# Seven raw weight buffers and eleven split ones, splits at most six steps ahead, load buffers at multiples of 256 bytes

## The chip, the cores and the metric

The kernel runs on one core of a Trainium2 chip. Its time is that of one execution in device microseconds; several executions are timed and the median is given. Below, PE is TensorE, DVE is VectorE, ACT is ScalarE, POOL is GpSimd and SP is the engine whose queue issues most DMA transfers.

## The reference

Linear attention over 8 batches and 8 heads (576 tokens, 64 values a head, 128 features), whose 4,608 rows of 512 values then go through a mixture of experts (MoE): a skip gate, the best of 8 experts for each row that passes it, and two matrix products with a ReLU between them.

```python
def phi(x):
    proj = np.einsum('bhsd,df->bhsf', x, w_phi)
    proj = proj - np.max(np.abs(proj), axis=-1, keepdims=True)
    return np.concatenate([np.exp(proj), np.exp(-proj)], axis=-1)
q_p, k_p = (phi(q), phi(k))
kv = np.einsum('bhsf,bhsd->bhfd', k_p, v)
z = np.sum(k_p, axis=2)
num = np.einsum('bhsf,bhfd->bhsd', q_p, kv)
den = np.einsum('bhsf,bhf->bhs', q_p, z)[..., None] + 1e-06
attn = num / den
...
do_compute = x @ w_skip > 0
xc = x[do_compute]
e_idx = np.argmax(xc @ w_gate, axis=1)
h = np.maximum(xc[mask] @ w1[e], 0.0)          # for each expert e, mask = its rows
y[mask] = gate_w[mask, None] * (h @ w2[e])
out[do_compute] = xc + y
```

Everything is fp32. A product of two fp32 matrices is made on PE of three products: each operand is split into a high part (`hi`, a copy rounded to PE's fp32r type) and the low rest (`lo` = value − `hi`), and hi·hi, hi·lo and lo·hi are summed.

## The kernel before

**Attention** takes the first 404 us or so. For each batch and pair of heads, q, k and v come in by SP's DMAs (`raw`, `v` and `vt`), DVE transposes part of the input (`xTt`, L301), PE makes the features, and the finished rows leave from `xm` (or `xt`) to the DRAM array `xrows` and to the output. A program's SBUF is handed out pool by pool in the order in which the pools are opened; attention's pools are closed before the MoE's open, so that the MoE's buffers lie over attention's.

**The MoE** works through ten slots, in the order E, E, E, C, C, S beside C, C, D beside S, C, D. E and D hold 256 rows, C 192, S 128. For each slot eight chunks of 512 KB of weights go past: four of w1, with which the slot's hidden values are made, and four of w2, with which its outputs are. One slot with one chunk is a *step*, 96 in all, numbered in PE's order. What happens to chunk k:

- **Load.** `fetch` (L181) issues one DMA on SP's queue (L188 for w1, L191 for w2) into one of four raw buffers, number k mod 4. So load k waits until the split of chunk k−4 has read its buffer.
- **Split.** `split` (L194) takes one of twelve pairs, number k mod 12: ACT copies the chunk to the high half (L199), and then DVE in one instruction, or POOL in four, subtracts to make the low half (L204). It waits until PE has finished step k−12.
- **Use.** `mm1` (L903, L916, L917, L919: w1) or `mm2` (L922 on, L930: w2), for S slots `half1` and `half2` (L855).

Around a step lies other work. `gather_rows` (L217) fetches a slot's rows from `xrows` by a POOL transfer; `rows` turns them on PE (L790) and ACT and DVE make their high and low halves (L793, L794). Hidden values are split by ACT (L808, L818) and DVE (L809, L820); for C slots ACT and DVE first empty the PSUM bank into `hsum` (L908, L909); for S slots ACT makes `hr` (L838) and PE turns it (L844). At a slot's end DVE makes the output rows `o` (L877, L888, L889) and their indices `si` (L862), and POOL scatters them (L863). Hidden values have three PSUM banks (`ps_P`) and one more (`ps_K`), transposes two (`ps_U`), outputs two (`ps_O`).

Each engine works through its queue in order. The order is written out by hand, in the loop over steps: at step k the loop first emits the splits that are due, each with the load of the chunk four further, and then step k's products. How far ahead splits go is set by a small planner (`T`, `ready`, `parted`), which estimates when a step starts and when a chunk has been loaded and split:

```python
while nxt < len(steps) and nxt <= k + 8 and (nxt <= k + 1 or parted[nxt] <= T[k] + 1.0):
```

So a split stands at most eight steps ahead of its use. Which engine subtracts is fixed: DVE, except for chunks 1 and 3 of w1 of a C slot, chunks 1 and 3 of an S slot, and a list for the E slots, which are POOL's.

Of the kernel before, what the change touches and what calls it, by code (L numbers as in the profile page):

```python
# [8 lines left out]
F32 = mybir.dt.float32  # L9
F32R = mybir.dt.float32r  # L10
BF16 = mybir.dt.bfloat16
I32 = mybir.dt.int32
# [5 lines left out]

P = 128
SLOT = 256  # L20
CFG = {'late': 1, 'gp': (0, 1, 2, 4, 6, 8, 9, 11, 12, 14, 17, 19, 21), 'rows': 9.0, 'tab': (2, 4, 5, 6, 6, 7, 8, 9, 10, 11, 12, 13, 16, 20, 32), 'ql': -2, 'q1': 0, 'vtl': 3, 'at': 6, 'cp': 0, 'ini': 'vvpvppvvpvp', 'inz': '', 'seq': ('E', 'E', 'E', 'C', 'C', 'SC', 'C', 'DS', 'C', 'D'), 'lag': (1, 3, 4, 5, 6), 'post': (4, 5, 7), 'man': (8, 79), 'dnow': 0, 'off': 6, 'order': 'EPAZUT', 'direct': (), 'nb': {'K': 1, 'P': 3, 'U': 2, 'O': 2}, 'apools': (('ld', 2), ('hl', 5), ('up', 5), ('zp', 2), ('ep', 7), ('kvp', 6), ('ac', 1), ('xp', 2)), 'mpools': (('rawp', 1), ('mx', 2), ('wseta', 1), ('mo', 2), ('wsetb', 1), ('wsetc', 1))}


@with_exitstack
def kernel(
# [13 lines left out]
    B, H, S, D = q.shape  # L39
    NF = w_phi.shape[1]  # L40
    E = w_gate.shape[1]
# [22 lines left out]
    const = ctx.enter_context(tc.tile_pool(name="const", bufs=1))  # L64
# [5 lines left out]
    pools = {}  # L70
    for nm, bufs in CFG["apools"]:
        pools[nm] = actx.enter_context(tc.tile_pool(name=nm, bufs=bufs))
    ac = pools["ac"]
    NB = CFG["nb"]
    DIRECT = CFG["direct"]

# [9 lines left out]
    nc.vector.memset(warm, 0.0)  # L86
    nc.scalar.activation(out=warm, in_=warm, func=AF.Exp)

    wsrc = ac.tile([P, NF], F32, name="wsrc")
    own = ac.tile([P, 2], F32, name="own")  # L90
    nc.vector.memset(own, 0.0)
    for dh in range(2):
        for hd in range(2):
# [17 lines left out]
    ones_f = const.tile([P, 32], F32, name="ones_f")  # L111
    iota_p = const.tile([P, P], F32, name="iota_p")

    vts = [ac.tile([P, 2, 2, D], F32, name="vt%d" % j) for j in range(2)]
    for vt in vts:
        nc.gpsimd.memset(vt, 0.0)
    desc = const.tile([P, E], F32, name="desc")
# [9 lines left out]
    eid0 = const.tile([1, 3], I32, name="eid0")  # L127
    idg0 = const.tile([P, 3, 2], I32, name="idg0")
    pad0 = const.tile([P, 3, 2], I32, name="pad0")
    mark = const.tile([1, 1], I32, name="mark")  # L130

    ft = const.tile([P, NSL, 4], I32, name="ft")

# [42 lines left out]
    wpool = []  # L176
# [2 lines left out]
    NFC = FF // FC  # L179

    def fetch(which, wap, c):  # L181
        rawp = wpool[0]
        i = nchunk[0]
        nchunk[0] += 1
        raw = rawp.tile([P, 1024], F32, tag="wraw%d" % (i % 4), name="wraw_c", bufs=1)
        if which == 1:
            src = wap[:, :, c * FC:(c + 1) * FC].rearrange("o (k p) f -> p (o k) f", p=P)
            nc.sync.dma_start(out=raw.rearrange("p (k f) -> p k f", f=FC), in_=src)  # L188
        else:
            src = wap[:, c * FC:(c + 1) * FC, :].rearrange("o (k p) m -> p (o k) m", p=P)  # L190
            nc.sync.dma_start(out=raw.rearrange("p (k m) -> p k m", m=DM), in_=src)  # L191
        return which, i, raw

    def split(chunk, eng):  # L194
        which, i, raw = chunk
        s = i % 12
        pair = wpool[1 if s < 4 else 2 if s < 9 else 3].tile([P, 2, 1024], F32R, tag="w%d" % s, name="w", bufs=1)
        hi, lo = pair[:, 0], pair[:, 1]
        nc.scalar.activation(out=hi, in_=raw, func=AF.Copy)  # L199

        n = 256 if eng is nc.gpsimd else 1024
        for a in range(0, 1024, n):
            r = slice(a, a + n)
            eng.tensor_tensor(out=lo[:, r], in0=raw[:, r], in1=hi[:, r].bitcast(F32), op=ALU.subtract)  # L204
        w = FC if which == 1 else DM
        return hi.rearrange("p (k f) -> p k f", f=w), lo.rearrange("p (k f) -> p k f", f=w)
# [24 lines left out]
    with actx:  # L231
        ld, hl, zp, up, ep, kvp, xp = (pools[nm] for nm in ("ld", "hl", "zp", "up", "ep", "kvp", "xp"))
# [55 lines left out]
        def st_t(u, i):  # L288
# [13 lines left out]
            else:  # L302
                nc.vector.transpose(out=xT.rearrange("p (g q c) -> p q g c", g=4, q=4), in_=src)
            nc.scalar.activation(out=hi, in_=xT, func=AF.Copy)  # L304
            nlo[0] += 1
            (nc.vector if CFG["ini"][nlo[0] - 1:nlo[0]] == "v" else nc.gpsimd).tensor_tensor(  # L306
                out=lo, in0=xT, in1=hi.bitcast(F32), op=ALU.subtract)
            u.hlp[(i + 1) // 2] = (hi, lo)

        def st_proj(u, i):  # L310
# [14 lines left out]
            if u.kind == "k" and i in DIRECT:  # L325
                nm = small.tile([P, 4], F32, tag="nm", name="nm")
                nc.vector.tensor_scalar(out=nm, in0=m, scalar1=-1.0, scalar2=None, op0=ALU.mult)
                u.u[i] = (pv, m, nm)
                if CFG["dnow"]:
                    st_exp_k(u, i)  # L330
# [9 lines left out]
        def st_exp_k(u, i):  # L340
# [22 lines left out]
            nz[0] += 1  # L363
            zeng = nc.vector if CFG["inz"][nz[0] - 1:nz[0]] == "v" else nc.gpsimd
            zeng.tensor_tensor(out=z, in0=e[:, 0:2, :], in1=e[:, 2:4, :], op=ALU.add)  # L365
# [343 lines left out]
        n = len(streams[0][0])  # L709
# [32 lines left out]
        man = None  # L742
        for t in range(n + OFF + LA):
            if CFG["man"] and t == CFG["man"][0]:
                man = ExitStack()
# [30 lines left out]
    pools = {}  # L776
    for nm, bufs in CFG["mpools"]:
        pools[nm] = ctx.enter_context(tc.tile_pool(name=nm, bufs=bufs, reuse_waits="tile"))
    wpool += [pools[x] for x in ("rawp", "wseta", "wsetb", "wsetc")]
    mxp, mo = pools["mx"], pools["mo"]  # L780

    def split_rows(xg, pad):
# [319 lines left out]
    def weight_regs(e):  # L1102
        r = nc.sync.value_load(e, min_val=0, max_val=E - 1)
        return bass.ds(r, 1)
# [3 lines left out]
    steps = []  # L1108
    cnt = dict(start)
    for grp in CFG["seq"]:  # L1110
# [7 lines left out]
        for which, w, n in how:  # L1118
            for _ in range(n):
                x = slots[which]  # L1120
# [7 lines left out]
    order = sorted(begin, key=begin.get)  # L1128
    raws, wts = {}, {}

    def load(k):
        if k < len(steps):
            w, x, c = steps[k]
            if w == 1 and c == 0:
                kind, i = x
                regs[x] = weight_regs((eid0 if kind == "E" else eid)[0:1, i:i + 1])
            raws[k] = fetch(w, (w1, w2)[w - 1][regs[x]], c)

    def part(k, eng):
        if k < len(steps):  # L1140
            wts[k] = split(raws.pop(k), eng)
# [11 lines left out]
    FIRST = 4  # L1153
    LATE = CFG["late"]
    took = {"E": 2.85, "D": 2.85, "C": 2.4, "S": 1.45}
    T, ready, parted = [], [], []
    for k, (w, x, c) in enumerate(steps):
        arrive = 0.0 if k < FIRST else max(ready[k - 1] + (3.0 if k < 12 else 2.35), parted[k - 4] + 4.0)
        ready.append(arrive)
        parted.append(max(arrive, T[k - 12] + 3.0 if k >= 12 else 0.0, parted[k - 1] + 1.25 if k else 0.0))  # L1160
        T.append(max(T[k - 1] + took[steps[k - 1][1][0]] + (1.0 if w == 1 and c == 0 else 0.0) if k else 2.0,
                     parted[k] + 2.5))

# [6 lines left out]
    def at(k, f):  # L1170
        along.append((k, f))
# [32 lines left out]
    with tc.manual_schedule():  # L1204
        nxt = FIRST
        for k in range(FIRST, FIRST + 4):
            load(k)
        rests[1]()
        for k, (w, x, c) in enumerate(steps):
            kind, i = x  # L1210
            for f in [f for s, f in before if s == k]:
                f()
            tabled[0] = kind != "E"
            todo = [f for s, f in along if s == k]
            while nxt < len(steps) and nxt <= k + 8 and (nxt <= k + 1 or parted[nxt] <= T[k] + 1.0):
                w_, x_, c_ = steps[nxt]
                v = nxt not in CFG["gp"] if x_[0] == "E" else not (
                    (x_[0] == "C" and w_ == 1 or x_[0] == "S") and c_ % 2 == 1)
                part(nxt, nc.vector if v else nc.gpsimd)
                load(nxt + 4)  # L1220
                nxt += 1
            if w == 1:
                if kind == "S":
                    st = hss.setdefault(x, {})
                    half1(wts[k], xss[x], c, st)
                    if c % 2 == 1:
                        st[c // 2] = half1_out(st[c // 2], c // 2)

                        def turn(st=st, g=c // 2):
                            st[g] = half1_turn(st[g])  # L1230
                        at(k + 1, turn)
                else:
                    hss.setdefault(x, []).append(mm1(wts[k], xss[x]))
            else:
                if c == 0:
                    ys[x] = [bank("O") for _ in range(1 if kind == "S" else 2)]
                if kind == "S":
                    half2(wts[k], ys[x][0], hss[x], c)
                elif x != last:
                    mm2(wts[k], ys[x], xss[x], hss[x], c)  # L1240
                elif c == NFC - 1:
                    for sub in range(2):
                        for cc in range(NFC):
                            mm2(wts[at_step[2, x, cc]], ys[x], xss[x], hss[x], cc, (sub,))
                        put(ys[x], xss[x], sub)
                if c == NFC - 1 and x != last:
                    def out_rows(x=x):
                        for sub in range(len(ys[x])):
                            if x[0] == "S":
                                store(ys[x][0], xss[x], 0)  # L1250
                            else:
# [53 lines left out]
```

## Time and profile before

| what | value |
|---|---|
| time, median of 3 runs | 670.46 us (670.17 to 672.61) |
| the profiled execution | 674.0 us, span 672.2 us |
| mean granted TensorE clock | 0.976 |
| MoE part in the span | about 404 to 662 us |
| DMA share, mean rate | 161 GB/s over the span |
| weight loads | 96 of 512 KB, median 4.7 us from issue to landing |

A row of a view names line, engine and operation, then the output buffer, an arrow and the inputs. A row of the timeline starts with its start and its duration; in square brackets stands how long its engine had been idle before it, and what ended that. A row of waits names who waited for whom, the total in us, the number of times and the longest. In the clock line each of 40 digits is a slice of 16.8 us, in tenths of full speed.

### The profile page before, as it was taken

The page shows a single profiled execution, that of the slowest core. Times are in us where ns is not written, and L with a number is a line of the kernel's source. Part 1 is how long each engine was busy: PE and PEld are TensorE (multiplying, and loading weights), DVE is VectorE, ACT ScalarE, POOL GpSimd, SP SyncE. Part 2 cuts the span into 40 slices and gives each one's busy share as a digit, 9 for nine tenths or more (in the row PEclk, how much of TensorE's full clock was granted, in tenths as well). Part 3 has the DMA queues.
Part 4 walks back from the last instruction along what each step waited for, and adds up shares of the span by engine and source line. Part 5 has one row for each costly group of instructions (what it writes and reads, how often), then busy time and mean ns, then how long its engine had stood idle before and what let it go on. Part 6 is the DMA issues. An engine that isn't in the chain of part 4 may idle for free. (4 is left out here: it accounts for less than half of the span.)

```text
span 672.2 us, 16380 instructions
## 1 busy us (share of the span) xinstructions
PE 600.2 (89%) x6046; PEld 513.3 (76%) x6046; DVE 519.9 (77%) x1245; ACT 372.9 (55%) x747; POOL 444.7 (66%) x484
## 2 busy tenths in 40 slices
PE   3897999979998989988899999869989897999894
PEld 2585887768887768777787898759978777988793
DVE  6868787888886987968999679995887776855750
ACT  4666665646655566656565643344656654655620
POOL 6896778677796687677688355887448845478011
PEclk9997999999999999999999999789999998999998
DMA  9889675765766585754403678568885768677710
GB/s 133 126 137 158 106 165 110 139 139 95 165 123 121 125 148 86 171 115 82 127 33 108 203 199 242 165 202 251 270 256 193 232 227 282 201 263 221 245 45 27
DMA packets 221685, 108.18 MB, mean 161 GB/s; under 512 B 160293, under 2 KB 202405, under 8 KB 221604
## 3 DMA queue, kind: packets, MB, share of 16 engines
q1 hardware_dynamic: 218272, 97.60, 59.7%
q0 software_dynamic: 3200, 9.45, 4.1%
q8 instruction: 49, 0.80, 0.5%
q14 instruction: 32, 0.26, 0.1%
q10 hardware_dynamic: 132, 0.07, 0.0%
HBM read 83.86 MB, written 24.02 MB: 160 GB/s over the span
## 5 line engine op out<-in xcount | busy, mean ns | idle before, releaser
L204 POOL TENSOR_TENSOR w<-wraw_c,w 128x256 fp32r<-128x256 f32 x124 | 111.0, 928 | 40.8 <-ACT w L199 40.6
L199 ACT ACTIVATE w<-wraw_c 128x1024 fp32r<-128x1024 f32 x96 | 100.2, 1056 | 61.8 <-DMA wraw_c<-in_moe_w_dram 55.9
L365 POOL TENSOR_TENSOR z<-ek 128x512 f32<-128x512 f32 x64 | 81.7, 1277 | 56.5 <-ACT ek L357 43.6
L204 DVE TENSOR_TENSOR w<-wraw_c,w 128x1024 fp32r<-128x1024 f32 x65 | 85.6, 1327 | 22.2 <-ACT w L199 22.1
L324 DVE TENSOR_REDUCE m<-ps_P 128x4 f32<-128x512 f32 (+1 forms) x160 | 96.6, 621 | 5.3 <-PE ps_P L320 5.1
L333 DVE TENSOR_TENSOR u<-ps_P,m 128x512 f32<-128x512 f32 (+1 forms) x160 | 96.0, 622 | 0.5
L318 PE MATMUL ps_P<-wph,hi 128*128 128x256 f32 x256 | 80.5, 314 | 16.7 <-ACT hi L304 8.7
L498 PEld LDWEIGHTS ps_O<-kva,eq 128*64 128x64 f32 x2048 | 75.2, 138 | 18.6 <-ACT eqt L385 7.1
L498 PE MATMUL ps_O<-kva,eq 128*64 128x74 f32 x2048 | 78.6, 229 | 5.6 <-ACT eqt L385 3.8
L306 POOL TENSOR_TENSOR lo<-xT,hi 128x512 fp32r<-128x512 f32 x61 | 78.1, 1280 | 5.5 <-ACT hi L304 5.2
L863 POOL DMA_INDIRECT out_dram<-o,si x22 | 26.7, 1214 | 73.3 <-DVE si L862 55.9
L320 PE MATMUL ps_P<-wph,lo 128*128 128x256 f32 x256 | 73.3, 286 | 0.0
L400 PE MATMUL ps_K<-ek,v 128*64 128x256 f32 x512 | 71.2, 395 | 1.9 <-DMA v<-in_v_dram 1.9
L319 PE MATMUL ps_P<-wpl,hi 128*128 128x256 f32 x256 | 72.9, 285 | 0.0
L384 ACT ACTIVATE eq<-ps_U 128x512 f32<-128x512 f32 x64 | 38.0, 594 | 57.2 <-PE ps_U L378 50.6
L930 PE MATMUL ps_O<-w,hh 128*128 128x512 f32 x160 | 64.6, 404 | 1.1 <-DVE o L877 1.1
L318 PEld LDWEIGHTS ps_P<-wph,hi 128*128 128x128 f32 x256 | 49.4, 193 | 21.1 <-ACT hi L304 8.9
L319 PEld LDWEIGHTS ps_P<-wpl,hi 128*128 128x128 f32 x256 | 49.8, 195 | 0.0
L320 PEld LDWEIGHTS ps_P<-wph,lo 128*128 128x128 f32 x256 | 49.2, 192 | 0.2 <-DVE lo L306 0.2
L301 DVE STREAM_TRANSPOSE xTt<-raw 128x128 f32<-128x128 f32 x32 | 9.9, 310 | 50.9 <-DMA raw<-in_k_dram 28.1
L378 PE MATMUL ps_U<-ident,u 128*128 128x128 f32 x288 | 48.4, 286 | 0.8 <-DVE u L333 0.8
L400 PEld LDWEIGHTS ps_K<-ek,v 128*64 128x64 f32 x512 | 32.0, 137 | 21.0 <-issue 5.4
(277 smaller groups left out, 1551.5 us busy)
## 6 DMA issues: line engine op xcount, KB each, us to landing
wraw_c<-in_moe_w_dram SPq DMA_DIRECT2D x96, 512.0 KB, 4.7
raw<-in_k_dram SPq DMA_DIRECT2D x64, 144.0 KB, 4.1
raw<-in_q_dram SPq DMA_DIRECT2D x64, 144.0 KB, 4.1
v<-in_v_dram SPq DMA_DIRECT2D x64, 128.0 KB, 3.7
out_dram<-xm SPq DMA_DIRECT2D x32, 256.0 KB, 4.1
xrows<-xm SPq DMA_DIRECT2D x8, 516.0 KB, 4.6
xrows<-xm SPq DMA_DIRECT2D x8, 512.0 KB, 5.2
vt<-in_v_dram SPq DMA_DIRECT2D x64, 16.0 KB, 3.0
```

Source lines behind the costliest of these rows:

```text
L199: nc.scalar.activation(out=hi, in_=raw, func=AF.Copy)
L204: eng.tensor_tensor(out=lo[:, r], in0=raw[:, r], in1=hi[:, r].bitcast(F32), op=ALU.subtract)
L306: (nc.vector if CFG["ini"][nlo[0] - 1:nlo[0]] == "v" else nc.gpsimd).tensor_tensor(out=lo, in0=xT, in1=hi.bitcast(F32), op=ALU.subtract)
L318: nc.tensor.matmul(o, hi[:, c], wph, start=True, stop=False)
L319: nc.tensor.matmul(o, hi[:, c], wpl, start=False, stop=False)
L320: nc.tensor.matmul(o, lo[:, c], wph, start=False, stop=True)
L324: nc.vector.tensor_reduce(out=m[:, 0:nt], in_=pv, axis=AX.X, op=ALU.max, apply_absolute_value=True)
L333: nc.vector.tensor_tensor(out=uu[:, 0:nt, :], in0=pv, in1=m[:, 0:nt].rearrange("p (t o) -> p t o", o=1).broadcast_to([P, nt, NF]), op=ALU. ...
L365: zeng.tensor_tensor(out=z, in0=e[:, 0:2, :], in1=e[:, 2:4, :], op=ALU.add)
L400: nc.tensor.matmul(o[hd * 64:hd * 64 + 64, :], u.v[:, 2 * pr + hd, g * D:(g + 1) * D], u.e[i][:, 2 * j + hd, :], start=(g == 0), stop=False,)
L498: nc.tensor.matmul(ov[s * 64:s * 64 + 64, 2 * j + hd, :], e[:, half, j, hd, s * 64:s * 64 + 64], kva[:, half, 2 * pr + hd, :], start=(half ...
L930: nc.tensor.matmul(y[sub], hh[:, t], wh[:, fi, :], start=first, stop=False)
```

## The change

**Raw buffers.** There are seven from load 12 on. The three new ones are a pool of their own (`rawq`), opened last, so that it lies over rows that attention's last stores (`xm` and its like) read. Loads 12 to 14 are the first to use them. A load waits for the split seven chunks earlier, and is emitted with the split of chunk k−7; with the split of chunk 7 go loads 11 to 14 at once.

**Split pairs.** Eleven in place of twelve; a split waits for PE's step eleven earlier. Splits stand at most six steps ahead of their use, not eight, and the planner's two formulas follow.

**Places in SBUF.** `own` and `mark` take 32 columns of which the first two and the first one are used as before, and `vts` is allocated earlier. The buffers behind them move: those of `raw`, `v`, `x`, `hi`, `lo`, `u` and the first four of `wraw_c` from 160 to 0 modulo 256 bytes. The three new raw buffers and four of the split pairs stand at 64, `xm` moves from 0 or 32 to 192 or 224, and the gathered rows `xg` from 0, 32, 64, 96 and 128 to 96, 128, 160, 192 and 224; `vt` stays at 0.

```diff
-    own = ac.tile([P, 2], F32, name="own")
+    own = ac.tile([P, 32], F32, name="own")[:, 0:2]
+    vts = [ac.tile([P, 2, 2, D], F32, name="vt%d" % j) for j in range(2)]
...
-    mark = const.tile([1, 1], I32, name="mark")
+    mark = const.tile([1, 32], I32, name="mark")[:, 0:1]
...
     def fetch(which, wap, c):
-        rawp = wpool[0]
         i = nchunk[0]
+        j = i % 4 if i < 12 else (i - 8) % 7
+        rawp = wpool[0 if j < 4 else 4]
         nchunk[0] += 1
-        raw = rawp.tile([P, 1024], F32, tag="wraw%d" % (i % 4), name="wraw_c", bufs=1)
+        raw = rawp.tile([P, 1024], F32, tag="wraw%d" % j, name="wraw_c", bufs=1)
...
     def split(chunk, eng):
-        s = i % 12
+        s = i % 11
...
-    wpool += [pools[x] for x in ("rawp", "wseta", "wsetb", "wsetc")]
+    wpool += [pools[x] for x in ("rawp", "wseta", "wsetb", "wsetc", "rawq")]
...
-        arrive = 0.0 if k < FIRST else max(ready[k - 1] + (3.0 if k < 12 else 2.35), parted[k - 4] + 4.0)
+        arrive = 0.0 if k < FIRST else max(ready[k - 1] + (3.0 if k < 12 else 2.35), parted[k - (4 if k < 12 else 7)] + 4.0)
         ready.append(arrive)
-        parted.append(max(arrive, T[k - 12] + 3.0 if k >= 12 else 0.0, parted[k - 1] + 1.25 if k else 0.0))
+        parted.append(max(arrive, T[k - 11] + 3.0 if k >= 11 else 0.0, parted[k - 1] + 1.25 if k else 0.0))
...
-            while nxt < len(steps) and nxt <= k + 8 and (nxt <= k + 1 or parted[nxt] <= T[k] + 1.0):
+            while nxt < len(steps) and nxt <= k + 6 and (nxt <= k + 1 or parted[nxt] <= T[k] + 1.0):
...
                 part(nxt, nc.vector if v else nc.gpsimd)
-                load(nxt + 4)
+                for n in (range(nxt + 4, nxt + 5) if nxt < 7 else range(11, 15) if nxt == 7 else range(nxt + 7, nxt + 8)):
+                    load(n)
                 nxt += 1
```

PE's order does not change at all, and up to about step 21 nor does that of the other engines. Behind it, splits stand about two steps later. Three places show it. In these rows a line number of the kernel after is 3 above that of before (L207 for L204), and "x4" is one split of POOL's, four instructions.

POOL, in the first C slots: a split, then the gather of a later slot's rows, then another split and the scatter of finished rows. Before:

```order
L204 TENSOR_TENSOR w<-wraw_c,w 128x256 x4
L217 DMA xg<-xrows,ft 128x514
L217 DMA xg<-xrows,ft 64x514
L204 TENSOR_TENSOR w<-wraw_c,w 128x256 x4
L863 DMA out_dram<-o,si 4608x512
L872 MEMSET mark 1x1
```

And after the change, at the same place:

```order
L220 DMA xg<-xrows,ft 128x514
L220 DMA xg<-xrows,ft 64x514
L207 TENSOR_TENSOR w<-wraw_c,w 128x256 x8
L866 DMA out_dram<-o,si 4608x512
L875 MEMSET mark 1x1
```

The split of chunk 33 stood ahead of the gather and now stands behind it.

POOL, near the end, where the splits of the slots S, C and D in steps 75 to 83 meet the scatters of a C slot and the gather of D's rows. Before:

```order
L217 DMA xg<-xrows,ft 64x514
L204 TENSOR_TENSOR w<-wraw_c,w 128x256 x16
L863 DMA out_dram<-o,si 4608x512
L872 MEMSET mark 1x1
L863 DMA out_dram<-o,si 4608x512
L872 MEMSET mark 1x1
L204 TENSOR_TENSOR w<-wraw_c,w 128x256 x4
L217 DMA xg<-xrows,ft 128x514 x2
```

After:

```order
L220 DMA xg<-xrows,ft 64x514
L207 TENSOR_TENSOR w<-wraw_c,w 128x256 x12
L866 DMA out_dram<-o,si 4608x512
L875 MEMSET mark 1x1
L866 DMA out_dram<-o,si 4608x512
L875 MEMSET mark 1x1
L207 TENSOR_TENSOR w<-wraw_c,w 128x256 x4
L220 DMA xg<-xrows,ft 128x514 x2
L207 TENSOR_TENSOR w<-wraw_c,w 128x256 x4
```

Four splits stood ahead of the scatters and one ahead of the gather behind them; now it is three ahead of the scatters, one between, and one behind that gather.

DVE, at the first step of the fourth C slot, which begins with the last rows of the slot before (`o`, `si`). Before:

```order
L877 SCALAR_TENSOR_TENSOR o<-ps_O,xg 128x512
L862 TENSOR_TENSOR si<-xg,ft 128x1
L888 SCALAR_TENSOR_TENSOR o<-ps_O,xg 64x512
L889 SCALAR_TENSOR_TENSOR o<-yl,xg,o 64x512
L862 TENSOR_TENSOR si<-xg,ft 64x1
L204 TENSOR_TENSOR w<-wraw_c,w 128x1024 x2
L909 TENSOR_TENSOR hsum<-ps_P,hsum 128x192
L909 TENSOR_TENSOR hsum<-ps_K,hsum 128x192
```

After:

```order
L880 SCALAR_TENSOR_TENSOR o<-ps_O,xg 128x512
L865 TENSOR_TENSOR si<-xg,ft 128x1
L891 SCALAR_TENSOR_TENSOR o<-ps_O,xg 64x512
L892 SCALAR_TENSOR_TENSOR o<-yl,xg,o 64x512
L865 TENSOR_TENSOR si<-xg,ft 64x1
L207 TENSOR_TENSOR w<-wraw_c,w 128x1024
L912 TENSOR_TENSOR hsum<-ps_P,hsum 128x192
L912 TENSOR_TENSOR hsum<-ps_K,hsum 128x192
```

Two splits stood between the output rows and the hidden values that PE waits for; now it is one.

More of the change, by code (lines that the diff above doesn't have):

```diff
@@ L20 @@
 SLOT = 256
-CFG = {'late': 1, 'gp': (0, 1, 2, 4, 6, 8, 9, 11, 12, 14, 17, 19, 21), 'rows': 9.0, 'tab': (2, 4, 5, 6, 6, 7, 8, 9, 10, 11, 12, 13, 16, 20, 32), 'ql': -2, 'q1': 0, 'vtl': 3, 'at': 6, 'cp': 0, 'ini': 'vvpvppvvpvp', 'inz': '', 'seq': ('E', 'E', 'E', 'C', 'C', 'SC', 'C', 'DS', 'C', 'D'), 'lag': (1, 3, 4, 5, 6), 'post': (4, 5, 7), 'man': (8, 79), 'dnow': 0, 'off': 6, 'order': 'EPAZUT', 'direct': (), 'nb': {'K': 1, 'P': 3, 'U': 2, 'O': 2}, 'apools': (('ld', 2), ('hl', 5), ('up', 5), ('zp', 2), ('ep', 7), ('kvp', 6), ('ac', 1), ('xp', 2)), 'mpools': (('rawp', 1), ('mx', 2), ('wseta', 1), ('mo', 2), ('wsetb', 1), ('wsetc', 1))}
+CFG = {'late': 1, 'gp': (0, 1, 2, 4, 6, 8, 9, 11, 12, 14, 17, 19, 21), 'rows': 9.0, 'tab': (2, 4, 5, 6, 6, 7, 8, 9, 10, 11, 12, 13, 16, 20, 32), 'ql': -2, 'q1': 0, 'vtl': 3, 'at': 6, 'cp': 0, 'ini': 'vvpvppvvpvp', 'inz': '', 'seq': ('E', 'E', 'E', 'C', 'C', 'SC', 'C', 'DS', 'C', 'D'), 'lag': (1, 3, 4, 5, 6), 'post': (4, 5, 7), 'man': (8, 79), 'dnow': 0, 'off': 6, 'order': 'EPAZUT', 'direct': (), 'nb': {'K': 1, 'P': 3, 'U': 2, 'O': 2}, 'apools': (('ld', 2), ('hl', 5), ('up', 5), ('zp', 2), ('ep', 7), ('kvp', 6), ('ac', 1), ('xp', 2)), 'mpools': (('rawp', 1), ('mx', 2), ('wseta', 1), ('mo', 2), ('wsetb', 1), ('wsetc', 1), ('rawq', 1))}
 @with_exitstack
@@ L112 @@
     iota_p = const.tile([P, P], F32, name="iota_p")
-    vts = [ac.tile([P, 2, 2, D], F32, name="vt%d" % j) for j in range(2)]
     for vt in vts:
```

## The prediction

> **What bounds the kernel now.** I read the page's busy shares and its clock line first, then three windows of the MoE part (404 us to the end), then the waits of TensorE there, then the chain behind the longest wait.
>
> ```profile
> PE 600.2 (89%) x6046; PEld 513.3 (76%) x6046; DVE 519.9 (77%) x1245; ACT 372.9 (55%) x747; POOL 444.7 (66%) x484
> PEclk9997999999999999999999999789999998999998
> 404.00:458.00 54.00, 46.12 (x300) 39.40 (x299) 49.30 (x101) 21.70 (x25) 39.54 (x45) 0.87 0.66 210
> 458.00:640.00 182.00, 169.56 (x1026) 151.31 (x1023) 132.56 (x208) 108.16 (x167) 105.58 (x118) 0.99 0.75 240
> ```
>
> A window row gives its length, then the busy time of PE, PE's weight load, DVE, ACT and POOL, the granted clock, the DMA share and GB/s. TensorE is the bound. From 404 to 458 us DVE is almost as full (49.30 of 54.00); from 458 to 640 us nothing but PE is (169.56 of 182.00), with the DMA engines at 0.75. What can be won there is PE's idle time:
>
> ```profile
> PE ps_P L903 <- DVE hsum L909: 6.7, 3, 3.9
> PE ps_P L917 <- DVE x L794: 3.1, 1, 3.1
> PE ps_P L919 <- POOL w L204: 2.4, 4, 1.3
> PE ps_P L916 <- ACT x L793: 2.0, 1, 2.0
> PE ps_U L790 <- DMA xg<-xrows,ft: 1.8, 2, 1.6
> PE ps_U L844 <- ACT hr L838: 1.7, 2, 1.4
> PE ps_O L930 <- DVE o L877: 1.1, 1, 1.1
> PE ps_O L855 <- DVE hlo L809: 1.0, 1, 1.0
> ```
>
> (total, times, longest). These sum to 19.8 us. None names a weight transfer, so I ask what the named engines waited for. The waits of ACT and of SP's queue from 404 to 663 us say it (L191 issues half of the loads, L188 the rest):
>
> ```profile
> ACT w L199 <- DMA wraw_c<-in_moe_w_dram: 55.9, 35, 7.0
> SPq L191 <- POOL w L204: 66.8, 18, 8.3
> ```
>
> A load may not be issued until the split four chunks earlier has emptied its raw buffer, and where that split is POOL's it ends late. The longest PE wait shows the whole chain:
>
> ```profile
> 551.74 7.20 SPq L191 DMA_DIRECT2D wraw_c<-in_moe_w_dram  x3
> 553.66 4.87 POOL L204 TENSOR_TENSOR w<-wraw_c,w 128x256 fp32r<-128x256 f32 x4
> 562.12 1.06 ACT L199 ACTIVATE w<-wraw_c 128x1024 fp32r<-128x1024 f32 x1 [2.86 <-DMA wraw_c<-in_moe_w_dram]
> 563.21 1.23 DVE L204 TENSOR_TENSOR w<-wraw_c,w 128x1024 fp32r<-128x1024 f32 x1 [1.90 <-ACT w L199]
> 564.35 0.35 DVE L909 TENSOR_TENSOR hsum<-ps_P,hsum 128x192 f32<-128x192 f32 x1
> 564.76 1.63 PE L903 MATMUL ps_P<-x,w 128*128 128x384 f32 x4 [3.94 <-DVE hsum L909]
> 564.80:568.20 3.40, 3.40 (x12) 3.40 (x13) 2.49 (x6) 1.91 (x4) 0.48 (x1) 0.50 1.08 358
> ```
>
> POOL's split of chunk 59 ends at 558.5; the third of SP's issues (load 63) goes out just then; ACT gets the chunk at 562.1; DVE subtracts it; only behind that subtraction does DVE empty the hidden bank (L909) that PE needs. That bank was ready long before: DVE stood 1.90 us at a split not yet due, with due work queued behind. After the gap the granted clock is 0.50 for 3.40 us, in which half the speed, 1.7 us, is lost.
>
> **The change part by part.** No arithmetic, no transfer and no instruction is added or removed: 96 loads, 96 ACT copies, the same DVE and POOL subtractions, PE's order untouched. The zeroing of `own` and the write of `mark` still touch two columns and one.
>
> *Seven raw buffers.* From load 12 on a load waits for the split seven chunks back. Load 63 then waits for split 56, which the row at 544.49 below shows done at 545.7, and can go out up to 13 us earlier than now. The transfers can follow: the last row above shows 358 GB/s while several loads are in flight, at which 512 KB last 1.5 us, below the 2.4 us that the planner allots to a C step. The same change covers each place where ACT or DVE stood at a late chunk:
>
> - at 564.8: 3.94 and 1.7 of clock, 5.6.
> - at 623.9 and 627.2 (below), the same chain behind POOL's split 83, and load 87 behind it: 2.02 and 0.75, 2.8. The clock line has no dip there (its slices 37 and 38 read 9), so nothing more.
>
> ```profile
> 612.93 4.83 POOL L204 TENSOR_TENSOR w<-wraw_c,w 128x256 fp32r<-128x256 f32 x4
> 621.30 1.06 ACT L199 ACTIVATE w<-wraw_c 128x1024 fp32r<-128x1024 f32 x1 [3.80 <-DMA wraw_c<-in_moe_w_dram]
> 623.94 0.98 PE L903 MATMUL ps_P<-x,w 128*128 128x384 f32 x4 [2.02 <-DVE hsum L909]
> 627.24 0.96 PE L903 MATMUL ps_P<-x,w 128*128 128x384 f32 x4 [0.75 <-DVE hsum L909]
> ```
>
> - ACT's hr (L838) behind the late chunks 49 and 51: 1.7, all of that row.
> - DVE's o (L877), which stood behind the subtraction of chunk 56, itself 1.53 us late: 1.1, all of it.
>
> ```profile
> 544.49 1.23 DVE L204 TENSOR_TENSOR w<-wraw_c,w 128x1024 fp32r<-128x1024 f32 x1 [1.53 <-ACT w L199]
> ```
>
> - hlo (L809) of DVE: half of its 1.0, so 0.5. The other half comes from a slow DVE instruction ahead of it, 2.90 us beside a POOL split, and 0.43 six us later:
>
> ```profile
> 533.69 2.90 DVE L820 SCALAR_TENSOR_TENSOR hlo<-hsum,hh 128x256 fp32r<-128x256 f32 x1 [0.59 <-ACT hh L818]
> 539.65 0.43 DVE L820 SCALAR_TENSOR_TENSOR hlo<-hsum,hh 128x256 fp32r<-128x256 f32 x1 [0.59 <-ACT hh L818]
> ```
>
> "SBUF — State Buffer" of the Trainium skill (section "Who interferes with whom") says that a DVE instruction with two SBUF inputs and a GpSimd instruction that reads SBUF contend, the later one being held; this pair of rows agrees. The change keeps both engines' splits, so such a meeting may fall elsewhere: 2.5 us a time by the two rows, on the path only where PE waits.
>
> - L793 and L794 at 447 to 455 us, 2.0 and 3.1. ACT's x stood behind hi 18 and 19, late by raw; but DVE is full there with the gate tables, and idle just 0.70 us for a chunk:
>
> ```profile
> 445.53 1.67 DVE L204 TENSOR_TENSOR w<-wraw_c,w 128x1024 fp32r<-128x1024 f32 x1 [0.70 <-ACT w L199]
> ```
>
>   I take 0.7, between nothing (DVE full) and 5.1 (all of it).
> - POOL's w (L919), four small waits at 425 to 429 us, stays, as does its half clock:
>
> ```profile
> 422.47 1.08 POOL L863 DMA_INDIRECT out_dram<-o,si  x1 [5.17 <-DVE si L862]
> 428.30:435.10 6.80, 6.29 (x22) 5.36 (x22) 6.42 (x15) 1.54 (x2) 6.31 (x8) 0.50 0.39 141
> ```
>
>   The split waits behind a scatter there, whose indices DVE had not made, and none of that moves: the order on all engines is unchanged up to about step 21.
>
> *Six steps ahead and eleven pairs.* From step 21 on each split stands about two steps later among the other work of ACT, DVE and POOL. One gain: the gather of 487.62 comes ahead of split 33.
>
> ```profile
> 484.33 3.14 POOL L204 TENSOR_TENSOR w<-wraw_c,w 128x256 fp32r<-128x256 f32 x4 [2.33 <-ACT w L199]
> 487.62 1.79 POOL L217 DMA_INDIRECT xg<-xrows,ft  x1 [0.15 <-issue]
> 494.13 0.66 PE L790 MATMUL ps_U<-ident,xg 128*128 128x128 f32 x4 [1.63 <-DMA xg<-xrows,ft]
> ```
>
> It is issued 2.33 + 3.14 us sooner, which covers PE's 1.63 and the second small wait of that group: 1.8.
> At C3's first step DVE's two L909 stand behind one split instead of two, which points the same way as the 5.6 above.
> The cost: POOL's splits 47, 81 and 83 fall behind scatters or gathers that they preceded, with 0 to 3 us between the forecast end of the split and PE's use. Where one comes late, the rows of 425 give the price: 2.4 of waits, and at most half of 6.80, 3.4, of clock, so 0 to 5.8 us each. Nothing below zero: moving a split behind other work cannot bring it forward. I take one such place without the clock, 2.4, nearest to the L919 row, since the clock fell after the gap at 564.8 and not after those at 494 and 624.
> Eleven pairs cost nothing: the split for step k+6 reuses the pair of step k−5, which PE has left; the cover is the reach of six steps.
>
> *Place of the new buffers.* Loads 12 to 14 need rows that attention's last stores still read. A store of that kind takes 5.2 us, load 12 goes out at 414.37 now, and POOL's subtraction of chunk 12 is the second half of its row of 7.49:
>
> ```profile
> xrows<-xm SPq DMA_DIRECT2D x8, 512.0 KB, 5.2
> 414.37 3.33 SPq L191 DMA_DIRECT2D wraw_c<-in_moe_w_dram  x2
> 424.88 7.49 POOL L204 TENSOR_TENSOR w<-wraw_c,w 128x256 fp32r<-128x256 f32 x8
> ```
>
> Held by a whole store, the load would go out at 419.6 and land by the same 5.2 at 424.8, still ahead of 428.6, the middle of that row: nothing.
>
> *Multiples of 256 bytes.* The raw buffers of attention, v and four of the weight buffers move to 0 mod 256 bytes; the three new ones stand at 64, and attention's output rows, sources of stores, move from 0 or 32 to 192 or 224. No two rows of this trace differ in alignment alone. The nearest:
>
> ```profile
> 10.00:30.00 20.00, 16.27 (x103) 11.92 (x104) 16.02 (x32) 13.21 (x28) 14.75 (x13) 0.91 1.11 155
> 51.50 0.31 DVE L301 STREAM_TRANSPOSE xTt<-raw 128x128 f32<-128x128 f32 x1 [4.53 <-DMA raw<-in_k_dram]
> 59.60:350.00 290.40, 266.54 (x3510) 224.17 (x3510) 242.84 (x687) 176.19 (x416) 218.70 (x208) 1.00 0.61 123
> ```
>
> The start of attention is limited by transfers (1.11), and one wait for raw is 4.53 us. The fourth digit of the clock line (50 to 67 us) is a 7: 0.7 to 0.8 of 16.8 us, so 3.4 to 5.0 are lost behind that wait. From 59.6 on transfers take 0.61 of the engines. So quicker loads could give up to 4.53 + 3.4, 8 us, and slower stores take as much; I take 0, the value nearest to the long last row, where PE is busy 266.54 of 290.40 us and transfers have room either way.
> "DMA: Bandwidth & Descriptors" (section "How a descriptor splits into AXI transactions") says that a read must start on a 256-byte boundary and that an unaligned one fetches bytes that nobody wants: 576 bytes at offset 224 take 25 beats and not 18. Here this speaks against the change, for it is the stores' sources in SBUF that leave the boundary. No run here shows it yet; by its kind of count, a store row of 1,024 bytes would cost about a sixth more, still beside PE's work.
>
> **Sum.** 5.6 + 2.8 + 1.7 + 1.1 + 0.5 + 0.7 + 1.8 = 14.2, less 2.4: 11.8 us off the profiled execution's 674.0 (its span is 672.2), 662.2. The median of the three times is 670.46, so the same share gives 670.46 × 662.2 / 674.0 = 658.7.
>
> **The rivals.**
> *Alignment pays too.* The 8 us above on top: 651. For it speaks that attention's start waits for raw; against it that the long stretch from 59.6 to 350 us has no use for quicker transfers.
> *The gain is halved.* DVE, 132.56 busy of 182.00, meets POOL more often, or the chunk is no longer late but the engine's order is: a second place, at 5.8 beside the 2.4, leaves 6.0 off: 664.5.
> *Nothing changes.* PE's waits shift to the next work in the queues: three POOL places at 5.8, 17.4, against the 14.2 removed leave 3.2 more, 673.6. This is also the change not doing what it says: the loads come early and the splits are made late, so that buffers, not engines, are early.
> *Slower: POOL's order.* From four such places on, 23.2 − 14.2 = 9 us, about 679. Candidates are 47, 49, 81 and 83, so all would have to miss; against it, POOL is idle 76 of 182 us in that window.
>
> **Chances.** Forecast (655 to 663.5) 0.56; alignment too (below 655) 0.10; halved (663.5 to 667.1) 0.12; within 0.5% of before, about what a measurement here can tell from no change (667.1 to 673.8), 0.13; slower 0.09. Faster is then 0.56 + 0.10 + 0.12 = 0.78. The range leaves out some 0.05 below and 0.13 above: from 651, the alignment case, to 669.
>
> **What would show it.** Right: ACT's wait for weight loads falls from 55.9 to under 20, and SP's waits for POOL too; no PE wait for L909 near 564 or 624 us; clock 1.00 there; the first 404 us and the waits at 425 to 455 alike within 1 us; the gather's wait at 494 gone. Wrong: PE waits for POOL's w from 515 us on or at 600 to 612, or L204 on DVE growing above its mean of the page through more meetings with POOL; attention shorter or longer by over 2 us would put alignment back into the sum.

## The result and the profile after

The changed kernel takes 651.78 us (median of 4 runs, 650.79 to 652.47) beside 671.54 for the kernel before (the three times of the table ahead and a fourth of 676.14): ratio 0.9693, 95% interval 0.9642 to 0.9744. The forecast was 658.7, a ratio of 0.9825. The profiled executions have spans of 649.6 and 672.2 us, 22.6 apart; that is more than the 19.8 between the medians, since the profiled execution before, 674.0 us, is one of its longer ones. The head of the page after, and its clock line:

```profile
span 649.6 us, 16375 instructions
...
PE 597.7 (92%) x6046; PEld 513.1 (79%) x6046; DVE 521.3 (80%) x1245; ACT 369.8 (57%) x747; POOL 451.5 (70%) x484
...
PEclk9898999999999989999999999898999999999998
```

PE is busy 2.5 us less with the same 6,046 products, and for a larger share of a shorter span. The dip that the clock line before had at 555 us is gone.

First I ask where the 22.6 us lie. A row that tells it is that of attention's output products (line 498, after the change 501): duration in ns as minimum, median and maximum, then the start of the first and of the last. Before, and then after:

```profile
L498 PE MATMUL ps_O<-kva,eq x2048: 225/227/384, 39.9 to 396.4; 128*64 128x74 f32 x187
```

```profile
L501 PE MATMUL ps_O<-kva,eq x2048: 225/227/385, 38.1 to 383.3; 128*64 128x74 f32 x187
```

The last one starts 13.1 us earlier: so much came from attention, whose order no engine changed. By the tenth transposition of raw, at 63.90 us before and 62.04 after, 1.9 us of them were won; the rest, 11.2, came behind it. What follows took 275.8 us before (672.2 − 396.4) and 266.3 after: 9.5 came from the MoE. Both parts gained; the forecast had 0 and 11.8.

In attention the DMA issues of the page show what became quicker (KB each, median us from issue to landing; before, and then after):

```profile
raw<-in_k_dram SPq DMA_DIRECT2D x64, 144.0 KB, 4.1
raw<-in_q_dram SPq DMA_DIRECT2D x64, 144.0 KB, 4.1
v<-in_v_dram SPq DMA_DIRECT2D x64, 128.0 KB, 3.7
out_dram<-xm SPq DMA_DIRECT2D x32, 256.0 KB, 4.1
```

```profile
raw<-in_k_dram SPq DMA_DIRECT2D x64, 144.0 KB, 3.4
raw<-in_q_dram SPq DMA_DIRECT2D x64, 144.0 KB, 3.3
v<-in_v_dram SPq DMA_DIRECT2D x64, 128.0 KB, 3.0
out_dram<-xm SPq DMA_DIRECT2D x32, 256.0 KB, 3.2
```

All four land 0.7 to 0.9 us sooner, among them the stores from `xm`, whose place became less regular. Their landing does not tell what that place is worth, though: it is 4.5 us in the second run below, where `xm` stands as in the changed kernel, and 3.9 in the last one, where it stands as before. The stretch of attention from 60 to 300 us (columns as in the prediction's windows), before and after:

```profile
60.00:300.00 240.00, 220.92 (x2923) 186.14 (x2923) 198.03 (x564) 146.13 (x347) 180.12 (x173) 1.00 0.66 131
```

```profile
60.00:300.00 240.00, 230.25 (x3049) 194.14 (x3048) 206.95 (x585) 151.45 (x359) 188.19 (x179) 0.99 0.63 135
```

More work gets done in the same 240 us (3,049 products instead of 2,923), with a lower DMA share at a higher rate. The time shows in DVE's waits at the first transposition of each load (over the whole span; total, times, longest), before and after:

```profile
DVE xTt L301 <- DMA raw<-in_k_dram: 28.1, 14, 4.5
DVE xTt L301 <- DMA raw<-in_q_dram: 11.5, 10, 2.6
DVE xTt L301 <- DMA out_dram<-xt: 9.8, 3, 3.4
```

```profile
DVE xTt L304 <- DMA raw<-in_k_dram: 20.4, 13, 4.0
DVE xTt L304 <- DMA raw<-in_q_dram: 14.8, 11, 3.2
```

These are 49.4 us before and 35.2 after, 14.2 less; attention ends 13.1 earlier. The rows that name raw fell by 4.4 only, from 39.6 to 35.2. The row that names `xt` belongs with them: its three waits stand ahead of transpositions of raw, each where q's turn is between two of k, and a transposition reads raw and not `xt`. That these three waited for raw is concluded from this; the row itself does not show it.

In the MoE the waits of PE from 380 us on, after the change, answer to the list in the prediction:

```profile
PE ps_P L920 <- DVE x L797: 4.7, 1, 4.7
PE ps_P L906 <- DVE hsum L912: 2.5, 4, 1.2
PE ps_O L933 <- DVE o L880: 2.4, 1, 2.4
PE ps_P L922 <- POOL w L207: 1.9, 2, 1.3
PE ps_O L937 <- POOL w L207: 1.3, 1, 1.3
```

And those of ACT and SP's queue from 389 us on, for weights (after the change L191 issues the loads of w1 and L194 those of w2), with the row of w1 before (L188), which the prediction did not show, at the end:

```profile
ACT w L202 <- DMA wraw_c<-in_moe_w_dram: 10.1, 6, 3.2
...
SPq L191 <- POOL w L207: 57.6, 16, 8.3
SPq L194 <- POOL w L207: 31.3, 9, 7.0
```

```profile
SPq L188 <- POOL w L204: 27.2, 7, 7.1
```

ACT's waits for weight loads fall from 55.9 to 10.1 us, although a load now lands 5.9 us after its issue (median) and not 4.7. The waits for the gather, for hr and for hlo are gone; that for hsum is 2.5 and not 6.7. SP's queue still waits 88.9 us for POOL's splits where it waited 94.0 (66.8 + 27.2), only for buffers that are needed later; the longer of the two rows is now that of w1 and was that of w2.

### The profile page after: what moved, and what is told of

It reads as the page before. It is cut to its first block, busy times and chain, and to the rows that moved or that the text cites. A ratio compares the mean times of both kernels' runs of the same rounds, so it can differ in the third digit from the quotient of the medians.

```text
span 649.6 us, 16375 instructions
## 1 busy us (share of the span) xinstructions
PE 597.7 (92%) x6046; PEld 513.1 (79%) x6046; DVE 521.3 (80%) x1245; ACT 369.8 (57%) x747; POOL 451.5 (70%) x484
## 5 line engine op out<-in xcount | busy, mean ns | idle before, releaser
L207 POOL TENSOR_TENSOR w<-wraw_c,w 128x256 fp32r<-128x256 f32 x124 | 115.3, 963 | 41.3 <-ACT w L202 41.2
L202 ACT ACTIVATE w<-wraw_c 128x1024 fp32r<-128x1024 f32 x96 | 97.7, 1051 | 11.9 <-DMA wraw_c<-in_moe_w_dram 10.1
L207 DVE TENSOR_TENSOR w<-wraw_c,w 128x1024 fp32r<-128x1024 f32 x65 | 86.2, 1338 | 11.4 <-ACT w L202 10.6
L866 POOL DMA_INDIRECT out_dram<-o,si x22 | 28.9, 1312 | 55.7 <-DVE si L865 49.1
L933 PE MATMUL ps_O<-w,hh 128*128 128x512 f32 x160 | 64.1, 400 | 2.4 <-DVE o L880 2.4
L937 PE MATMUL ps_O<-w,hh 128*128 128x512 f32 x120 | 47.3, 395 | 1.3 <-POOL w L207 1.3
```

What stands on the lines that cost most here:

```text
L933: nc.tensor.matmul(y[sub], hh[:, t], wh[:, fi, :], start=first, stop=False)
```

## The experiments

**Which part of the change.** The first run has the buffers and not the places, the second the places and not the buffers.

```diff
-    own = ac.tile([P, 32], F32, name="own")[:, 0:2]
-    mark = const.tile([1, 32], I32, name="mark")[:, 0:1]
+    own = ac.tile([P, 2], F32, name="own")
+    mark = const.tile([1, 1], I32, name="mark")
...
```

> The changed kernel with `own`, `mark` and `vts` as before, so that every buffer of attention is back at its old place (raw and v at 160 mod 256): seven raw buffers, eleven pairs and six steps ahead alone. Theory A (the places of the load buffers gave attention's 13 us, the buffers gave the MoE's gain): attention ends where it did before, PE's first MoE products as late as in the kernel before, the MoE part 9 to 10 us shorter, about 662. Rival B (the MoE's gain was the places too, its loads having become quicker): about 671 and ACT's waits for weights still near 50 us. The forecast's own sum for this edit alone is 11.8 off: 659.

661.08 us (659.22 to 666.04), ratio 0.9834 [0.977, 0.9899]. Attention ends nearly as before:

```profile
L501 PE MATMUL ps_O<-kva,eq x2048: 225/227/384, 39.0 to 393.9; 128*64 128x74 f32 x187
```

The rest of its span of 664.3 us takes 270.4, 5.4 less than before instead of 9 to 10. But this profiled execution, 666.04 us, is the slowest of five; the other four took 659.22 to 661.36, near the 662 expected. The timeline shows where 5 us of it stayed (start, duration, engine, and in brackets the idle time ahead):

```profile
431.69 9.57 DVE L1071 TENSOR_TENSOR rx<-eq,ids 128x1116 bf16<-128x1116 bf16 x1
431.74 8.34 POOL L207 TENSOR_TENSOR w<-wraw_c,w 128x256 fp32r<-128x256 f32 x12
442.45 0.79 PE L937 MATMUL ps_O<-w,hh 128*128 128x512 f32 x1 [5.16 <-DVE w L207]
```

One DVE instruction of the gate tables, 1.32 us where it comes next in this trace, lasts 9.57 us, until 1.2 us after POOL's three splits next to it are done; the subtraction behind it comes late, and PE waits 5.16 us. In the changed kernel's trace the two do not meet so, and the times of the other four executions suggest that they did not meet so there either, which no trace shows. ACT's waits for weights are 19.4 us in this run.

The second run is the reverse: the kernel before with the two lines above as in the change, and `vts` allocated earlier.

> The kernel before with only `own`, `mark` and `vts` changed, so that raw, v and four weight buffers stand at 0 mod 256; four raw buffers, twelve pairs, eight steps ahead as before. Theory A: attention 13 us shorter and the MoE as before, about 658; if weight loads too gain by their place, some us less. Rival C (attention was not shortened by places but by something that differs from run to run): 671. The forecast's term for this edit was 0, its rival at most 8 us.

659.12 us (658.71 to 662.44), ratio 0.9828 [0.9759, 0.9897]:

```profile
L498 PE MATMUL ps_O<-kva,eq x2048: 225/227/387, 37.7 to 380.5; 128*64 128x74 f32 x187
```

Attention's whole gain is there (380.5), the rest takes 277.2 of the span of 657.7, about as long as the 275.8 before, and ACT's waits for weights are 52.2 us beside 55.9: the places alone do not give the MoE's gain (rival B). The two parts add up: 0.9834 × 0.9828 is 0.9665, and both together gave 0.9693.

**Which multiple.** The next two are the changed kernel with `mark` of 64 and of 48 columns, which shifts raw, v and what follows them.

> The changed kernel with `mark` twice as wide: raw, v and the first four weight buffers stand at 128 mod 256, the three new ones at 192. If a load needs a buffer at a multiple of 256 bytes, the 13 us of attention are lost again: about 665. If multiples of 64 (or 128) do, nothing is lost: 652.

> The changed kernel with `mark` of 48 columns: raw, v and the first four weight buffers stand at 64 mod 256, the new ones at 128. With multiples of 64 as the condition: 652; with 128: about 658 to 665; with 256: about 665.

648.32 us (646.43 to 650.1), ratio 0.9658 [0.9591, 0.9725], with raw at 128, and 660.51 (659.05 to 661.66), ratio 0.9828 [0.9762, 0.9894], with raw at 64. In the same order:

```profile
L501 PE MATMUL ps_O<-kva,eq x2048: 225/227/384, 37.8 to 381.0; 128*64 128x74 f32 x187
```

```profile
L501 PE MATMUL ps_O<-kva,eq x2048: 225/227/384, 40.0 to 392.8; 128*64 128x74 f32 x187
```

Multiples of 128 do; 64 modulo 128 loses nearly all of it, like 160 (32 modulo 128) in the kernel before. A multiple of 256 is not what is needed.

**Which buffer.** v alone is moved by 64 bytes, to the wrong remainder in the third run's kernel and to the right one in the fourth's.

```diff
-            u.v = ld.tile([P, 4, 4 * D], F32, tag="v", name="v")
+            u.v = ld.tile([P, 1088], F32, tag="v", name="v")[:, 16:1040].rearrange("p (a b) -> p a b", a=4)
```

> The third run's kernel (raw at 128 mod 256) with v alone moved by 64 bytes to 192 mod 256, which is 64 mod 128. If raw's place alone gave attention's gain: as the third run, 648, raw's median landing near 3.3 us. If v's place did: attention about 11 us longer, 659 to 660. If both share it: 650 to 657.

> The fourth run's kernel (raw at 64 mod 256) with v alone moved by 64 bytes to 128 mod 256. The mirror of the fifth run: raw alone matters: 660, raw landing near 4.0; v alone matters: 648 to 650; both: between.

647.94 us (645.77 to 649.42), ratio 0.9637 [0.9578, 0.9696], and 660.08 (659.51 to 661.26), ratio 0.9833 [0.9778, 0.9889]; attention's last product starts at 380.9 and at 392.6 us. v's place changes nothing; what remains is raw, or one of the buffers of attention that moved with it.

**Is it the limit of six steps?**

```diff
-            while nxt < len(steps) and nxt <= k + 6 and (nxt <= k + 1 or parted[nxt] <= T[k] + 1.0):
+            while nxt < len(steps) and nxt <= k + 8 and (nxt <= k + 1 or parted[nxt] <= T[k] + 1.0):
```

> The changed kernel with splits at most eight steps ahead again in place of six (seven raw buffers, eleven pairs and places as changed). If the limit of six matters by what stands ahead of the gather and of hsum in the queues (the forecast gave it 1.8 and a share of 5.6): 653 to 656, with PE's wait for the gather near 490 us back. If the seven raw buffers did it all: 652.

651.11 us (649.49 to 652.45), ratio 0.9686 [0.9631, 0.9741]: no different from six. The wait for the gather is back, as expected, but the one ahead of o's bank (L933) is 0.8 and not 2.4; the two roughly change places:

```profile
PE ps_U L793 <- DMA xg<-xrows,ft: 3.1, 2, 1.9
...
PE ps_O L933 <- DVE si L865: 0.8, 1, 0.8
```

**Do weight loads gain by their place too?** The third run's kernel, with the three new raw buffers and the later pairs at 0 and not at 192:

```diff
-        ixt = mo.tile([P, 4], I32, tag="ixt", name="ixt")
+        ixt = mo.tile([P, 16], I32, tag="ixt", name="ixt")[:, 0:4]
```

> The third run's kernel (raw, v and the first four weight buffers at 128 mod 256) with a small tile ahead of the later pools widened, so that the three new raw buffers and the seven later pairs stand at 0 mod 256 in place of 192. If weight loads gain by their place as attention's loads do: 1 to 3 us less than the third run, 645 to 647, the weight loads' landing shorter. If they land early enough anyway: 648.

648.96 us (647.36 to 650.29), ratio 0.9669 [0.9614, 0.9723], beside 648.32: no gain. ACT waits 9.3 us for weights there and 10.3 in the third run, little in both.

**What about the place costs.** raw is filled in pieces of 128 bytes, one beside the other. At 64 or 160 half of these pieces cross a multiple of 256 bytes, and all of them a multiple of 128; the two cannot be told apart so. In the next three runs the pieces stand 256 bytes apart (in two buffers instead of four, for lack of room); between the three only the start within the 256 bytes differs, and the order on all engines is the same.

```diff
-            u.raw = ld.tile([P, 2, 18, 32], F32, tag="raw", name="raw", bufs=4)
+            u.raw = ld.tile([P, 2368], F32, tag="raw", name="raw", bufs=2)[:, S:S + 2304].rearrange("p (a b c) -> p a b c", a=2, c=64)[:, :, :, 0:32]
...
```

S is 0, 16 and 48 values of 4 bytes: pieces at 0, 64 and 192. In the part left out DVE's first transposition reads the pieces at their new distance, alike in all three.

> The changed kernel with the 128-byte pieces of q and k, which stand side by side in raw, put 256 bytes apart, each at 0 mod 256; for lack of room raw then has two buffers instead of four. Base of this series: its attention will be longer for want of buffers, its packets as short as the changed kernel's (mean near 13.0 ns for 128 bytes).

> As the ninth run, with each piece at 64 mod 256: every piece crosses a multiple of 128 bytes, none a multiple of 256. If a write costs more where it crosses a multiple of 256 bytes (half of the pieces did so in the kernel before): as the ninth run. If it needs a multiple of 128: raw's waits and attention 8 us or more longer than in the ninth run.

> As the ninth run, with each piece at 192 mod 256: every piece crosses a multiple of 256 bytes. By both theories longer than the ninth run; if crossing 256 is what costs, by more than the kernel before lost, since all pieces cross and not half of them; if only 128 counts, by as much as the tenth run. If neither the tenth nor the eleventh is longer, it was not the pieces' places that cost.

652.48 us (651.42 to 654.67), 651.62 (649.74 to 652.99) and 700.96 (698.79 to 704.0); ratios 0.9715 [0.9659, 0.977], 0.9692 [0.9637, 0.9748] and 1.0435 [1.037, 1.05]. Attention's row for the three, in the same order:

```profile
L501 PE MATMUL ps_O<-kva,eq x2048: 225/227/278, 41.0 to 384.0; 128*64 128x74 f32 x187
```

```profile
L501 PE MATMUL ps_O<-kva,eq x2048: 225/227/278, 42.3 to 385.4; 128*64 128x74 f32 x187
```

```profile
L501 PE MATMUL ps_O<-kva,eq x2048: 225/227/333, 46.5 to 431.2; 128*64 128x74 f32 x187
```

Pieces that cross only a multiple of 128 cost nothing; pieces that all cross a multiple of 256 cost 46 to 47 us of attention. The expectation that two buffers make attention longer was wrong: 384.0 beside 383.3. The window from 60 to 300 us and DVE's wait for k, first of the tenth run and then of the eleventh:

```profile
60.00:300.00 240.00, 227.85 (x3036) 192.28 (x3032) 205.84 (x579) 150.27 (x353) 184.54 (x176) 1.00 0.61 133
```

```profile
DVE xTt L304 <- DMA raw<-in_k_dram: 16.4, 12, 2.0
```

```profile
60.00:300.00 240.00, 205.98 (x2592) 173.14 (x2592) 178.20 (x499) 132.51 (x313) 163.16 (x154) 0.96 0.77 116
```

```profile
DVE xTt L304 <- DMA raw<-in_k_dram: 36.0, 13, 3.9
```

The DMA share goes from 0.61 to 0.77 while the rate falls from 133 to 116 GB/s. All pieces crossing cost 46 us and half of them 13 in the kernel before; since the distance between pieces and the number of buffers differ too, this does not show by itself how the cost grows with the number of pieces.

The traces also keep every packet that the DMA engines moved, and packets of 128 bytes are raw's alone (147,456 in each trace). Their mean duration is 13.0 ns in all nine kernels whose pieces cross no multiple of 256 bytes, the tenth run's among them; 13.8 to 14.2 ns in the four in which half of the pieces cross one; and 20.0 ns in the eleventh run, where all do. So crossing lengthens raw's packets in the mean, but not each of them: the median is 13 ns in every trace, the eleventh run's too. Why some of the crossing packets last long and others do not stays open. DVE's first transposition of each load lasts 311 ns in the mean in the eleventh run and 310 before, so that reading raw there got no slower.

**raw alone, in the kernel before.**

```diff
-            u.raw = ld.tile([P, 2, 18, 32], F32, tag="raw", name="raw", bufs=4)
+            u.raw = ld.tile([P, 1216], F32, tag="raw", name="raw", bufs=4)[:, 24:1176].rearrange("p (a b c) -> p a b c", a=2, c=32)
```

> The kernel before with one edit: each of attention's four raw buffers is 256 bytes longer, and its values begin 96 bytes further in, at 0 mod 256; every other buffer keeps its place modulo 256, and the order on all engines is that of before. If 128-byte pieces of raw that cross a multiple of 256 bytes (half of them before, none now) are the whole cause of attention's 13 us: 655 to 659, like the second run. If the other buffers' places had a share: above 661.

663.33 us (655.68 to 664.81), ratio 0.9856 [0.9753, 0.9959]: slower than expected, and by the median alone the rival would hold. The four executions lie far apart, though: one took 655.68, as expected, and the profiled one, 664.81, is the slowest. The trace tells the parts apart, by attention's row, the landings and PE's longest wait in the MoE:

```profile
L498 PE MATMUL ps_O<-kva,eq x2048: 225/227/384, 38.0 to 381.8; 128*64 128x74 f32 x187
```

```profile
raw<-in_k_dram SPq DMA_DIRECT2D x64, 144.0 KB, 3.3
...
v<-in_v_dram SPq DMA_DIRECT2D x64, 128.0 KB, 3.1
```

```profile
PE ps_P L903 <- DVE hsum L909: 8.8, 4, 3.9
```

Attention has all of its gain (381.8 beside 396.4), with v, `xm` and every engine's buffers at their old places; v lands 0.6 us sooner though it did not move. The packets of 1,024 bytes, v's among them, last 54.8 ns in the mean in the first 300 us, and 69.2 before. The loss is in the MoE, 281.3 us of a span of 663.1 beside 275.8 before, with the same buffers and order; the waits for hsum are 8.8 instead of 6.7. Why the MoE with four raw buffers takes 276 to 281 us in these three traces stays open; the executions of this one kernel differ by more (655.68 to 664.81). With seven it took 264 to 268 in every trace but the first run's.

## Why the prediction was off

The direction was right and the size was not: 11.8 us forecast, 22.6 between the profiled spans.

- **Multiples of 256 bytes, the step that failed.** The term was 0 and measured 13.1 (15.9 from the kernel before to the second run, 10.6 from the first run to the changed kernel, pairs that differ in places alone). Even its outer bound, 8, was too small, for it counted only the start of attention, where 1.9 us were won, and took nothing from the long stretch behind it, where 11.2 were, on the ground that PE was busy 266.54 of 290.40 us and the DMA engines 0.61. That row was the wrong one to take the price from. A share of 0.61 says that the engines have room, not that a transfer's duration is hidden: the wait of 4.53 us was one of 24 for raw, 39.6 us in all (49.4 with the three put down to `xt`), and a landing 0.7 us sooner came back in pieces all along attention. That total was in the trace before, and is the row by which the term should have been bounded.
- **"Here this speaks against the change"**, said of the stores from `xm`. The prediction took the boundary of 256 bytes from reads, as "DMA: Bandwidth & Descriptors" of the Trainium skill (section "How a descriptor splits into AXI transactions") states it, and so looked for it at the stores' sources in SBUF and not where loads are written. The runs at 0, 64 and 192 show such a boundary on the written side of a load. The sixth that the prediction put on a store row (by that count a row of 1,024 bytes that starts at 192 takes an estimated 38 beats for 32, so nearer a fifth) does not show: the packets of 1,032 bytes, which only the stores to `xrows` have, last 47 ns in the median in all fourteen traces, wherever `xm` stands. Its premise was weak too: the rows of `xm` are 2,056 bytes apart and its buffers stood at 0 and 32, so that one row in eight started on the boundary before.
- **The rival "alignment pays too"** named 651 and was right in kind. That its time is so near to 651.78 is luck: it added 8 us at attention's start to 11.8 from the MoE, and the profiles show 13.1, mostly behind the start, and 9.5. It got a chance of 0.10 because its evidence was looked for in attention's first 60 us only.
- **Seven raw buffers**: right in mechanism. 9.5 us came from the MoE beside 11.8. The wait for hsum fell by 4.2 and the half clock behind it went, 5.9 of the forecast 8.4; hr 1.7, as forecast; hlo 1.0, forecast 0.5; x (L793, L794) 0.4, forecast 0.7. PE's waits and the half clock together account for 8.5 of the 9.5. That the seven buffers and not the eleven pairs bring this is read from ACT's waits; no run has the one without the other.
- **The wait for o (L930 before, L933 after)** was to fall from 1.1 to nothing and grew by 1.3 instead. The trace after shows why:

```profile
518.56 4.91 POOL L207 TENSOR_TENSOR w<-wraw_c,w 128x256 fp32r<-128x256 f32 x7
519.50 4.27 DVE L823 SCALAR_TENSOR_TENSOR hlo<-hsum,hh 128x256 fp32r<-128x256 f32 x1 [0.59 <-ACT hh L821]
523.89 4.62 DVE L207 TENSOR_TENSOR w<-wraw_c,w 128x1024 fp32r<-128x1024 f32 x4
528.43 0.74 DVE L880 SCALAR_TENSOR_TENSOR o<-ps_O,xg 128x512 f32<-128x512 f32 x1
529.22 0.50 PE L933 MATMUL ps_O<-w,hh 128*128 128x512 f32 x1 [2.45 <-DVE o L880]
```

  An instruction of DVE that lasted 0.43 us elsewhere takes 4.27 beside POOL's splits; four subtractions queue up behind it, and o comes behind them. The prediction had named this meeting, with 2.5 us "on the path only where PE waits", and left it out of the sum.
- **One new POOL place, 2.4**: in the changed kernel's trace PE does not wait for POOL's w at any of the splits that the prediction named. Its one new row of that kind, 1.3 at L937, lies at 427 us, and the second and the last run, with the order of before, have it too (L934, 1.3). That this and the 1.3 for o add to 2.6 is luck. In the fifth run's trace the wait for o is missing, and PE waits 2.4 us for POOL's w at 524 to 526 us (L909) instead: there such a place cost the 2.4 that was forecast. The waits for POOL's w (L922) stayed, 1.9 beside 2.4.
- **Six steps ahead**: 1.8 for the gather came, but the limit as a whole is worth nothing that these runs can tell (651.11 with eight): with eight the gather's 3.1 come back while the waits for o and others shrink, and PE's waits in the MoE add to 13.5 us beside 13.2.
- **Of the signs to look for**, ACT's waits (under 20) and the clock near 564 us held, and the gather's wait is gone. The waits for hsum near 564 and 624 us shrank but did not vanish: 1.2 and 0.8 us are left at 545 and 548 us, and 0.3 at 604. SP's waits for POOL hardly fell (88.9 beside 94.0), presumably because a queue that runs ahead stands at the next buffer whatever their number. "Attention alike within 1 us" failed, and the prediction had said what that would mean.

## What to carry to other kernels

Look at where small pieces of a load land: here pieces of 128 bytes that crossed a multiple of 256 bytes in SBUF delayed their own transfer and those beside it, and a few bytes of padding mended it. A low DMA share does not make a transfer's duration free; sum the waits for that transfer over the whole stage before a price of nothing is written down. When more buffers take one late arrival out of an in-order queue, look next at what the same queue meets instead.

## What the runs showed of the hardware

- The boundary is 256 bytes and not 128 (attention's end at 385.4 against 431.2 us for pieces of 128 bytes that cross the one or the other, their packets 13.0 against 20.0 ns), and it counts for the written side of a load. The cost is shared: v landed in 3.1 us instead of 3.7 when only raw moved.
- A two-input DVE instruction can be held by a whole row of POOL's instructions and not by one of them: 9.57 us instead of 1.32 beside twelve of them, 4.27 instead of 0.43 beside seven. By the trace the first of the two began 0.05 us ahead of POOL's row and was held all the same, where the prediction had the later one held; 0.05 us is too little to decide this.
- The kernels with raw at 128 took 648.32, 647.94 and 648.96 us, each a little under the changed kernel's 651.78; their intervals overlap its own, so they are not told apart from it here.
